# Asking for two spectrum buffers earlier: every buffer of the split weights moves by 2,112 bytes

## The chip, the cores and the metric

The kernel runs on one core of a Trainium2 chip. The metric is the device time of one launch in microseconds (us), as the median of several runs. Time within a run comes from one profiled execution, whose records give each instruction's engine, start and length. The engines are PE (TensorE: matmuls, with PEld its weight loads), DVE (VectorE), ACT (ScalarE), POOL (GpSimd) and SP (SyncE, which issues most of the DMAs). The on-chip memory SBUF has 128 partitions, and an address below is a byte offset within each partition.

## What is computed

The reference, cut to what matters (8 batches, 8 heads, 576 tokens, 64 values a head, 32 packed queries, model width 512):

```python
def sm_attn(qq, kk, vv):
    s = scale * qq @ kk.T;  a = exp(s - max(s));  return (a / (sum(a) + 1e-9)) @ vv

p_packed = sm_attn(p, k, v)                 # 32 packed rows per head
x = sm_attn(q, p_packed, p_packed)          # heads joined: [8, 576, 512]
u = x + real(fft(fft(x, axis=tokens), axis=width))
un = (u - mean(u)) / sqrt(var(u) + 1e-6)
out = u + relu(un @ w_ch1) @ w_ch2          # 512 -> 2048 -> 512
```

## The kernel before

**Two parts.** `front(b)` does attention, the two Fourier transforms (as matmuls with tables of waves) and the residual for batch b. `ffn` does the feed-forward part for a tile of 512 tokens. There are 8 batches and 9 tiles of tokens. `front(0)` runs ahead; from then on the front of the next batch is cut into steps (`yield`) that `step` puts between the halves of the current tile's feed-forward.

**The feed-forward part.** A tile has 16 steps over the hidden width, j = 0 to 15, and each has two halves, which this text calls up and down:

- `up(j)`, matmul line 804: 128 hidden rows for 512 tokens. PE loads a 128x128 piece of the weights (`wr_h` or `wr_l`) and streams 512 columns of the tokens past it (`uh` or `ul`): 4 pieces of the width times 3 products, 12 matmuls into one bank of PSUM (`ph`).
- `down(j - 1)`, matmul line 822: PE loads a 128x128 piece of the hidden rows (`hh` or `hl`) and streams 512 columns of weights past it (`wr_h` or `wr_l`): 4 groups of tokens times 3 products, 12 matmuls, each three of them into one of the four banks `acc0` to `acc3`.

Every number is kept as a sum of two parts of type fp32r, a high and a low one, so each product is made of three matmuls (high by high, high by low, low by high). Of the two operands of a matmul this text calls the one that is loaded the *loaded* operand, and the one that streams past it the *streamed* one. The split weights are the streamed operand of a down matmul and the loaded operand of an up matmul. In numbers, 9 tiles x 16 steps x 24 matmuls are 3,456 matmuls with 512 columns (the first `up` of the first tile is cut into two halves of 256 columns), 1,728 on each line.

**What feeds it.** `wsplits` splits the weights anew for every tile: ACT casts 128x512 of them to `wr_h` (line 99), POOL subtracts to get `wr_l` (line 100). Six buffers with the tag `wr` take turns. After an `up`, ACT writes `hh` (line 811) and DVE `hl` (line 812), two buffers each. `uh` and `ul` are one buffer each per tile of tokens, with 2,048 bytes for each of the four pieces.

**Where a buffer lies.** The pool `work` gives each tag its place in SBUF in the order in which tags are first asked for, one behind the other, each rounded up to 32 bytes. All of it happens while the program is written; nothing is placed while it runs. The order of the first requests around the change is: `xh`, `oh`, `fh`, `fl`, `xl`, `ol` (batch 0's folded attention weights), `yr0` and `yr1` in `wave_split` (line 565), `wr` in `wsplits` (line 776; the first request comes from `waves_of`, line 579), `spec0` and `spec1` in `spectrum` (line 591), then `ln` (`un`), `ul`, `hh`, `hl`. The tag `uh` comes much earlier, because `folded` (line 471) uses it for batch 0 under the name `f`. A `spec` buffer takes 1,032 bytes (258 columns), rounded up to 1,056; all buffers of the feed-forward part take multiples of 2,048.

`first_values` (line 603) is the step "X" of batch 0's order of work. It stands before the step "P1", in which `waves_of` runs `wave_split`, and so before the first requests for `yr0` and `wr`.

Of the kernel before, what the change touches and what calls it, by code (L numbers as in the profile page):

```python
# [9 lines left out]
F32 = mybir.dt.float32  # L10
# [7 lines left out]
P = 128  # L18
# [33 lines left out]
N2 = 258  # L52
# [25 lines left out]
def tile_kernel(ctx, tc, kpT, qT, v, w1, w2, tabs, tabR, tabB, tabT, sel, ident_d, out):  # L78
# [5 lines left out]
    work = ctx.enter_context(tc.tile_pool(name="work", bufs=2))  # L84
# [7 lines left out]
    def bank(name):  # L92
        nbank[0] += 1
        if nbank[0] % 7 < 4 and spare:
            return psf.tile([P, 512], F32, tag=spare[nbank[0] % 7], name=name)
        return ps.tile([P, 512], F32, tag="ps", name=name)
# [136 lines left out]
    def three(o, lh, ll, rh, rl, first, last):  # L233
        nc.tensor.matmul(o, lh, rh, start=first, stop=False)  # L234
        nc.tensor.matmul(o, lh, rl, start=False, stop=False)  # L235
        nc.tensor.matmul(o, ll, rh, start=False, stop=last)  # L236

    def front(b):
# [342 lines left out]
        def spectrum(t, par):  # L581

            pz = bank("pz")
            k0, off = (0, 0) if par is not None else (P, rows.start)
            pars = (0, 1) if par is None else (par,)
            for i, q in enumerate(pars):
                w = slice(KW * q + k0 - off, KW * q + k0 - off + P)
                three(pz[:, :N2], tbh[t][:, w], tbl[t][:, w], yh[t][:, q, :], yl[t][:, q, :], i == 0, False)
            k0 = KW * par if par is not None else k0
            nc.tensor.matmul(pz[:, :N2], tbr[t][:NRC[t], k0 - off:k0 - off + P], yr[t][:NRC[t]], start=False, stop=True)  # L590
            sb = work.tile([P, N2], F32, tag=f"spec{t}", name=f"spec{t}", bufs=1)
            nc.scalar.copy(sb, pz[:, :N2])
            return sb

        def value(ah, al, w):
            px = bank("px")
            for g in range(2):
                three(px[:, g * 256:(g + 1) * 256], ah[g][:, w], al[g][:, w], bdh[g], bdl[g], True, True)
            return px

        early = []

        def first_values():
            early.extend(value(h, l, slice(1, 256, 2)) for h, l in ((xh, xl), (oh, ol)))

        parts = {"S": lambda _: scores(0, 1), "s": scores, "q": queries, "U": lambda _: queries(0, 1), 
                 "t": turned_scores, "p": packed, "c": on_diagonal, "d": packed_parts, "l": packed_split,
                 "v": turned_queries, "X": lambda g: first_values() if b == 0 else turned_scores(0, 1), "e": less_one, "m": less_mean, "g": values_spectrum,
                 "G": values_products, "T": values_turned, "z": values_split, "a": weights, "w": scaled, "b": upright,
                 "f": folded, "r": folded_rest, "h": folded_parts, "x": values_rest, "P": waves_of,  # L610
# [46 lines left out]
        if b == 0:  # L657

            pq = None
            for c in range(2):  # L660
                px = early if c == 0 else [side_value(n, c) for n in range(2)]
                AB = spectrum(0, c), spectrum(1, c)
                if c == 1:
                    yield
                    for key in ((b, "E", 0), (b, "O", 0)):
                        rows_of(key, *pq)
                        statistics(key)
                        yield
                else:
                    yield  # L670
                pq = sums(c, lambda n: px[n], *AB)
# [6 lines left out]
        else:  # L678
            for c in range(2):
                A, Bs = spectrum(0, c), spectrum(1, c)  # L680
                yield
                pe, qe = sums(c, lambda n: side_value(n, c), A, Bs)
                for key in ((b, "E", c), (b, "O", c)):
                    rows_of(key, pe, qe)
                for key in ((b, "E", c), (b, "O", c)):
                    statistics(key)
                yield (None, "rest")[c]

        kr = (b // 2, "R")
        if b % 2 == 0:  # L690
            new_u(kr)
        rows = slice(0, D) if b % 2 == 0 else slice(D, P)
        A, Bs = spectrum(0, None), spectrum(1, None)
        yield
        px = value(fh, fl, slice(FA - rows.start, FA - rows.start + P))
# [180 lines left out]
    tiles = [(i, keys[i:i + 4]) for i in range(0, len(keys), 4)]  # L876

    gen0 = front(0)
    cur = Turned(tiles[0][1])
    ready, splits = [], wsplits()  # L880
# [38 lines left out]
    for t, (first, tk) in enumerate(tiles):  # L919

        gen = front(t + 1) if t + 1 < B else iter(())
        ended = []

        def step(i):

            next_step()

            k = i + 2 * LEAD
            if i in (0, 2):
                next(rest, None)  # L930
            elif not ended and next(gen, None) == "rest":
                ended.append(gen)
            if t == 0 and i > 0 and k <= 2 * NJ:
                joined((k - 1) // 2, (k - 1) % 2)
                if 8 < k + 2 < 2 * NJ:
                    fetch((k + 2) // 2, (k + 2) % 2)
            if t == 0 and k < 2 * NJ:
                halves_of(k // 2, k % 2)
            assert i < 2 * NJ - 1 or t + 1 >= B or ended

        nxt = Turned(tiles[t + 1][1]) if t + 1 < len(tiles) else None

        with tc.manual_schedule(engines=MANUAL):
            ffn(first, cur, step, nxt, t + 1 >= B, t + 1)
        cur, rest = nxt, gen
# [112 lines left out]
```

## Time and profile before

| | us |
|---|---|
| median of 3 runs | 998.75 (997.57 to 1001.8) |
| the profiled execution, whole | 999.18 |
| its span, first to last instruction | 997.4 |
| PE busy | 963.9 (97%) |
| weight loads (PEld) | 781.5 (78%) |
| DVE, ACT, POOL busy | 552.7, 473.9, 462.9 |

Matmuls are pipelined: a record of 390 to 400 ns runs from a matmul's start until its last result, while the next one starts some 230 ns after it. What a matmul costs in a row of matmuls is read from the distance between starts, and not from its mean length. In the chain of waits, a piece like "PE acc L822 x24" is a row of 24 matmuls, and its length divided by 24 is that distance.

### The profile page before, as it was taken

Reading aid. Unit: us, or ns where it says so; the run is one execution under the profiler, and the core shown is the slowest. Engines: PE = TensorE matmul, PEld = TensorE weight load, DVE = VectorE, ACT = ScalarE, POOL = GpSimd, SP = SyncE. Lnnn points to the kernel's source line nnn. Section 1 sums busy time; section 2 is a strip of 40 time slices with the busy share of each in tenths; the row PEclk is TensorE's granted clock in tenths of the full one; section 3 lists DMA queues with packets and bytes.
Section 4 is the critical chain, followed back from the end, with each engine's and each line's share of the span. In section 5 each row is a group of like instructions: output and inputs, shape, how many; then the busy total and the mean of one; then the engine's idle time right before and its main releaser. Section 6 shows DMA issues by size and latency. Waiting matters only on the chain.

```text
span 997.4 us, 14993 instructions
## 1 busy us (share of the span) xinstructions
PE 963.9 (97%) x5588; PEld 781.5 (78%) x5588; DVE 552.7 (55%) x1153; ACT 473.9 (48%) x957; POOL 462.9 (46%) x405
## 2 busy tenths in 40 slices
PE   4589999999999999999999999999999999999998
PEld 2567788788877887788878887788778888888886
DVE  5877865576546845585547654684549551123111
ACT  4687775444544445444534454444543443344331
POOL 2456544554445433643455444543455354444442
PEclk9799999999999999999999999999999999999999
DMA  9336543300140003101320024002310010011001
GB/s 367 105 131 193 156 134 103 112 1 1 47 143 26 1 14 128 49 1 47 104 86 1 16 77 143 1 2 60 129 48 1 22 65 1 1 35 50 1 1 43
DMA packets 28169, 65.93 MB, mean 66 GB/s; under 512 B 5494, under 2 KB 12992, under 8 KB 28096
## 3 DMA queue, kind: packets, MB, share of 16 engines
q1 hardware_dynamic: 27264, 63.79, 19.4%
q0 software_dynamic: 832, 1.18, 0.5%
q8 instruction: 44, 0.72, 0.3%
q14 instruction: 29, 0.24, 0.1%
HBM read 48.70 MB, written 9.44 MB: 58 GB/s over the span
## 4 chain that ended last, share of the span: by engine, by line
PE 90%; DVE 4%; ACT 3%; DMA 1%; issue 1%; POOL 1%; DVEq 0%; ACTq 0%; POOLq 0%
PE acc L822 38%; PE ph L804 38%; PE po L323 1%; PE py L236 1%; PE py L234 1%; PE py L235 1%; PE s L266 1%; PE px L236 1%; PE px L234 1%; PE px L235 1%; PE e1tp L300 1%; PE pz L234 1%; PE pz L236 1%; PE pz L235 1%; PE s2T L266 1%
## 5 line engine op out<-in xcount | busy, mean ns | idle before, releaser
L100 POOL TENSOR_TENSOR wr_l<-w1f,wr_h 128x512 fp32r<-128x512 f32 x144 | 192.6, 1337 | 294.2 <-ACT wr_h L99 254.8
L812 DVE SCALAR_TENSOR_TENSOR hl<-ph,hh 128x512 fp32r<-128x512 f32 (+1 forms) x145 | 99.6, 687 | 346.0 <-ACT hh L811 345.8
L100 POOL TENSOR_TENSOR wr_l<-w2f,wr_h 128x512 fp32r<-128x512 f32 x144 | 188.6, 1309 | 172.8 <-ACT wr_h L99 172.2
L804 PE MATMUL ph<-uh,wr_h 128*128 128x512 f32 (+1 forms) x580 | 230.3, 398 | 4.0 <-DVE hl L812 2.6
L822 PE MATMUL acc<-wr_h,hh 128*128 128x512 f32 x576 | 228.7, 397 | 0.0
L822 PE MATMUL acc<-wr_l,hh 128*128 128x512 f32 x576 | 228.2, 396 | 0.0
L822 PE MATMUL acc<-wr_h,hl 128*128 128x512 f32 x576 | 228.0, 396 | 0.0
L804 PE MATMUL ph<-uh,wr_l 128*128 128x512 f32 (+1 forms) x580 | 227.3, 392 | 0.0
L804 PE MATMUL ph<-ul,wr_h 128*128 128x512 f32 (+1 forms) x580 | 221.8, 391 | 0.0
L811 ACT ACTIVATE hh<-ph 128x512 fp32r<-128x512 f32 (+1 forms) x145 | 86.4, 596 | 215.7 <-PE ph L804 214.9
L804 PEld LDWEIGHTS ph<-uh,wr_h 128*128 128x128 f32 x580 | 109.1, 188 | 40.2 <-ACT gh L99 6.0
L822 PEld LDWEIGHTS acc<-wr_h,hl 128*128 128x128 f32 x576 | 108.1, 188 | 26.1
L804 PEld LDWEIGHTS ph<-uh,wr_l 128*128 128x128 f32 x580 | 108.9, 188 | 24.7
L822 PEld LDWEIGHTS acc<-wr_h,hh 128*128 128x128 f32 x576 | 108.1, 188 | 24.7
L822 PEld LDWEIGHTS acc<-wr_l,hh 128*128 128x128 f32 x576 | 108.1, 188 | 23.9
L804 PEld LDWEIGHTS ph<-ul,wr_h 128*128 128x128 f32 x580 | 108.7, 188 | 22.5
L99 ACT CAST wr_h<-w1f 128x512 fp32r<-128x512 f32 x144 | 89.1, 618 | 60.8 <-PE acc L822 53.9
L99 ACT CAST wr_h<-w2f 128x512 fp32r<-128x512 f32 x144 | 88.3, 613 | 13.4 <-PE acc L822 7.6
L234 PE MATMUL py<-gh,fh 128*128 128x258 f32 (+2 forms) x96 | 28.2, 294 | 13.6 <-ACT fh L99 13.6
L213 ACT ACTIVATE junk<-ubuf,stat 128x512 f32<-128x512 f32 x36 | 25.6, 714 | 24.9 <-DVE stat L209 24.9
L100 POOL TENSOR_TENSOR gl<-turned,gh 128x516 fp32r<-128x516 f32 x16 | 24.6, 1537 | 26.9 <-ACT gh L99 26.9
L217 POOL TENSOR_TENSOR stat<-stat,mhalf 128x1 f32<-128x1 f32 x36 | 24.3, 690 | 11.5 <-DVE stat L216 11.5
(186 smaller groups left out, 1229.5 us busy)
## 6 DMA issues: line engine op xcount, KB each, us to landing
kp<-kpT SPq DMA_DIRECT2D x16, 608.0 KB, 3.9
out<-ubuf SPq DMA_DIRECT2D x36, 256.0 KB, 2.1
vt<-v SPq DMA_DIRECT2D x14, 640.0 KB, 4.8
wst<-w SPq DMA_DIRECT2D x17, 512.0 KB, 3.9
qt<-qT SPq DMA_DIRECT2D x14, 576.0 KB, 5.1
raw<-flip SPq DMA_DIRECT2D x208, 32.0 KB, 1.8
ubuf<-w SPq DMA_DIRECT2D x9, 512.0 KB, 3.8
w1f<-w SPq DMA_DIRECT2D x3, 512.0 KB, 11.3
```

Source lines behind the costliest of these rows:

```text
L99: nc.scalar.copy(hi, src)
L100: (lo_eng or nc.vector).tensor_tensor(lo, src, hi.bitcast(F32), ALU.subtract)
L213: nc.scalar.activation(junk, u, AF.Square, bias=st[:, 1:2], scale=1.0, accum_out=st[:, 2:3])
L217: nc.gpsimd.tensor_tensor(st[:, 2:3], st[:, 2:3], mhalf, ALU.pow)
L234: nc.tensor.matmul(o, lh, rh, start=first, stop=False)
L235: nc.tensor.matmul(o, lh, rl, start=False, stop=False)
L236: nc.tensor.matmul(o, ll, rh, start=False, stop=last)
L266: nc.tensor.matmul(res[g][c][at, :w.stop - w.start], lhs(g, h), rhs(g, h, w), start=True, stop=True, tile_position=(r, h * NPK))
L804: nc.tensor.matmul(o[:, t], l[:, c * P:(c + 1) * P], r[:, c, t], start=(n == 0), stop=(n == 11))
L811: nc.scalar.activation(hh[:, t], o[:, t], AF.Relu)
L812: nc.vector.scalar_tensor_tensor(hl[:, t], o[:, t], 0.0, hh[:, t].bitcast(F32), ALU.max, ALU.subtract)
L822: nc.tensor.matmul(acc[i], l[:, w], r, start=(j == 0 and k == 0), stop=(j == NJ - 1 and k == 2))
```

## The change

`first_values` now asks for the two `spec` buffers, before `yr` and `wr` have been asked for, and keeps them in a dictionary; `spectrum` takes the buffer from there at its first use for each of the two, and asks the pool itself from then on, as before.

```diff
-            sb = work.tile([P, N2], F32, tag=f"spec{t}", name=f"spec{t}", bufs=1)
+            sb = specs.pop(t, None) or work.tile([P, N2], F32, tag=f"spec{t}", name=f"spec{t}", bufs=1)
             nc.scalar.copy(sb, pz[:, :N2])
             return sb
...
-        early = []
+        early, specs = [], {}
 
         def first_values():
+
+            specs.update((t, work.tile([P, N2], F32, tag=f"spec{t}", name=f"spec{t}", bufs=1)) for t in range(2))
             early.extend(value(h, l, slice(1, 256, 2)) for h, l in ((xh, xl), (oh, ol)))
```

No engine has an instruction more or less, and none stands in another place or waits for something else; only addresses differ. As the two programs are built, these are the addresses (bytes in a partition) and what is left of them after division by 2,048 and by 128:

| buffer | before | mod 2,048 | mod 128 | after | mod 2,048 | mod 128 |
|---|---|---|---|---|---|---|
| `uh` (4 x 2,048) | 161408 | 1664 | 0 | 161408 | 1664 | 0 |
| `spec0`, `spec1` | 204608, 205664 | 1856, 864 | 64, 96 | 190208, 191264 | 1792, 800 | 0, 32 |
| `yr0`, `yr1` | 190208, 191264 | 1792, 800 | 0, 32 | 192320, 193376 | 1856, 864 | 64, 96 |
| `wr` (6 x 2,048) | 192320 | 1856 | 64 | 194432 | 1920 | 0 |
| `un`, `ul`, `hh`, `hl` | 206720 and on | 1920 | 0 | 206720 and on | 1920 | 0 |

So of the feed-forward operands only the six `wr` buffers move. They then lie a multiple of 2,048 bytes from `ul`, `hh` and `hl`; `uh` lies 256 bytes off that grid before and after.

## Prediction

> **What bounds the kernel now.** I read the page first, then the chain of waits, then PE's waits, and last single starts of matmuls on the timeline. From the page, the span and the engines:
>
> ```profile
> span 997.4 us, 14993 instructions
> PE 963.9 (97%) x5588; PEld 781.5 (78%) x5588; DVE 552.7 (55%) x1153; ACT 473.9 (48%) x957; POOL 462.9 (46%) x405
> PE 90%; DVE 4%; ACT 3%; DMA 1%; issue 1%; POOL 1%; DVEq 0%; ACTq 0%; POOLq 0%
> PE acc L822 38%; PE ph L804 38%; PE po L323 1%; PE py L236 1%; PE py L234 1%; PE py L235 1%; PE s L266 1%; PE px L236 1%; PE px L234 1%; PE px L235 1%; PE e1tp L300 1%; PE pz L234 1%; PE pz L236 1%; PE pz L235 1%; PE s2T L266 1%
> ```
>
> The third and fourth lines are the chain that ended last, by engine and by line: 90% of it is PE, and the two feed-forward lines hold 38% each, some 760 of the 997.4 us. Next, who keeps PE waiting, and how busy the engines are in the middle (busy us of PE, PEld, DVE, ACT and POOL with their instructions, then the granted clock):
>
> ```profile
> PE py L234 <- ACT fh L99: 13.6, 1, 13.6
> PE s1t L266 <- DMA kp<-kpT: 4.7, 1, 4.7
> PE ph L804 <- DVE hl L812: 2.6, 3, 1.4
> ...
> 500.00:600.00 100.00, 100.00 (x578) 81.81 (x577) 63.45 (x132) 45.21 (x90) 50.21 (x42) 1.00 0.14 42
> ```
>
> The longest wait, 13.6 us, happens once, the next, 4.7 us, once as well, and no feed-forward line waits more than 2.6 us in all. In the middle PE has no idle time, at the full clock, while DVE, the busiest of those that feed it, is idle for a third of it. So the time of this kernel is the number of matmuls times the distance between their starts, and only what changes that distance can show. How many they are:
>
> ```profile
> L804 PE MATMUL ph<-uh,wr_h 128*128 128x512 f32 (+1 forms) x580 | 230.3, 398 | 4.0 <-DVE hl L812 2.6
> L822 PE MATMUL acc<-wr_h,hh 128*128 128x512 f32 x576 | 228.7, 397 | 0.0
> L822 PE MATMUL acc<-wr_l,hh 128*128 128x512 f32 x576 | 228.2, 396 | 0.0
> L822 PE MATMUL acc<-wr_h,hl 128*128 128x512 f32 x576 | 228.0, 396 | 0.0
> ```
>
> The down line has 3 x 576 = 1,728 matmuls, the up line the same number to within a dozen. Their mean length, 396 to 398 ns, says nothing about the distance. That stands in the longest pieces of the chain:
>
> ```profile
> 898.59 5.60 PE acc L822 x24
> 904.19 5.51 PE ph L804 x24
> ```
>
> 24 down matmuls take 5.60 us, 233.3 ns each; 24 up matmuls take 5.51 us, 229.6 ns each. That is the row on which the prediction rests: two kinds of matmul with the same columns, the same types, the same engine, without waits, and 3.7 ns between them. Inside one step (an up and the down behind it, starts in the first column; the rows left out are the matmuls between):
>
> ```profile
> 940.13 0.39 PE L804 MATMUL ph<-uh,wr_h 128*128 128x512 f32 x1
> ...
> 941.29 0.39 PE L804 MATMUL ph<-uh,wr_l 128*128 128x512 f32 x1
> ...
> 942.66 0.39 PE L804 MATMUL ph<-uh,wr_l 128*128 128x512 f32 x1
> 942.89 0.39 PE L822 MATMUL acc<-wr_h,hh 128*128 128x512 f32 x1
> 943.12 0.40 PE L822 MATMUL acc<-wr_l,hh 128*128 128x512 f32 x1
> 943.36 0.39 PE L822 MATMUL acc<-wr_h,hl 128*128 128x512 f32 x1
> 943.59 0.40 PE L822 MATMUL acc<-wr_h,hh 128*128 128x512 f32 x1
> 943.83 0.39 PE L822 MATMUL acc<-wr_l,hh 128*128 128x512 f32 x1
> ...
> 945.69 0.39 PE L804 MATMUL ph<-uh,wr_h 128*128 128x512 f32 x1
> ```
>
> From 940.13 to 942.89 are 12 up intervals, 230.0 ns each; the last six before 942.66, from 941.29 on, are 228.3 ns each, so an up starts slower and settles. From 942.89 to 945.69 are 12 down intervals, 233.3 ns. Not every up is that quick. In the middle of the run there is this one:
>
> ```profile
> 535.54 0.40 PE L804 MATMUL ph<-uh,wr_h 128*128 128x512 f32 x1
> ...
> 538.11 0.39 PE L804 MATMUL ph<-uh,wr_l 128*128 128x512 f32 x1
> ```
>
> Its 11 intervals are 233.6 ns each, the down's rate. So there are two rates, about 229 and about 233.4 ns; the down shows only the slow one, the up both.
>
> **The change, part by part.** No instruction is added, taken away or moved, so there is no cost of that kind. What can change is what an instruction costs at its new addresses.
>
> *The down matmuls.* They stream `wr`, which lies 64 bytes past a multiple of 128 now, and load `hh` or `hl`, which lie on one. The quick up matmuls stream `uh` and `ul`, which lie on a multiple of 128. What else tells the two apart is that a down changes its bank of PSUM every three matmuls, but its rows show no step there: from the third matmul at 943.36 to the fourth, in the next bank, it is 0.23 us, as it is from the first to the second. So I take the place of the streamed operand as the likeliest reason, and after the change it is on a multiple of 128 everywhere. Then the down runs at the rate of the piece with 24 up matmuls: 1,728 / 24 = 72 pieces, each 5.60 - 5.51 = 0.09 us shorter, 6.5 us. All of it is on the path, since PE is what everything waits for. Upper bound: all matmuls at the settled 228.3 ns, which is (233.3 - 228.3) x 1,728 = 8.6 us in the down and (229.6 - 228.3) x 1,728 = 2.2 us in the up, together 10.9 us. Lower bound under this reason: only half of the downs get there, as an up also runs slow at times: 3.2 us. I take 6.5, the value that a row of 24 shows.
>
> *The up matmuls.* They load `wr` and stream what hasn't moved. If it is the loaded operand's place that counts, they lose what they have: 72 pieces at 5.60 in place of 5.51, 6.5 us more at most, and less by those ups that are slow already. Under the reason above it is nothing.
>
> *The other readers and writers.* ACT and POOL write `wr`, at new addresses:
>
> ```profile
> L99 ACT CAST wr_h<-w2f 128x512 fp32r<-128x512 f32 x144 | 88.3, 613 | 13.4 <-PE acc L822 7.6
> L100 POOL TENSOR_TENSOR wr_l<-w2f,wr_h 128x512 fp32r<-128x512 f32 x144 | 188.6, 1309 | 172.8 <-ACT wr_h L99 172.2
> ```
>
> A step of 5.56 us (940.13 to 945.69) needs two of each, 2 x 0.61 us of ACT and 2 x 1.31 us of POOL, so both could get slower by half and would still hide behind PE. `yr` is the streamed operand of one line:
>
> ```profile
> L590 PE MATMUL pz<-yr,tbr x48: 280/284/288, 42.5 to 817.0; 101*128 101x258 f32 x24, 99*128 99x258 f32 x24
> ```
>
> 48 matmuls by a difference of the size seen above, 3.7 ns, are 0.2 us either way. `spec` is read by DVE, a third of whose time is free. Together I set these at nothing, with 0.2 us to either side.
>
> *A rule that speaks against the change.* The Trainium skill, page "SBUF — State Buffer", section "Who interferes with whom", says that PE has two independent read ports, one for the streamed operand and one for the weight load, and that PE never waits on anyone; it names no price for where an operand starts. By that rule the sum would be zero. The trace agrees in that PE has no idle time in the 100 us above, with DVE, ACT and POOL at work for 63, 45 and 50 us of them; whether it also holds for an operand's place no row of one program can show.
>
> *The sum.* The profiled execution took 999.18 us, its span 997.4 and 1.8 around it. 997.4 - 6.5 + 1.8 = 992.7. The median of the three runs is 0.43 below that execution, so the forecast is 992.3, rounded to 992.
>
> **The rivals.** A difference of about 0.5%, 5 us, is what a measurement of this kernel can tell from none.
>
> *The place is not the reason.* The two rates could be two ways in which the same loop of load and stream falls into step, as the slow up at 535.54 suggests: its addresses are those of any other up, but for which of the six `wr` buffers it loads. Then the down would be slow for another reason (three products in a bank and not twelve, or what it waits for at its first matmul), the rates stay, and the time is 998.75, between 997 and 1001. This is also the rule of the page above. For it speaks the slow up; against it that no down in the rows above is quick.
>
> *The change doesn't do what it says.* `uh` stays 256 bytes off the grid, and two of three up matmuls stream it. If all operands had to be on one grid, only the down and the `ul` matmuls would change. It gives a part of the first sum, 3 us or so, and I count it with no change.
>
> *Slower: what counts is how near the loaded operand lies to the streamed one.* In a down the two lie 64 bytes apart modulo 512, in an up 192 bytes (`wr` behind `uh`) or 64 bytes short of a whole 512 (`wr` behind `ul`); the down is the slow one. Afterwards a down and the `ul` matmuls have them at the same place modulo 512. If near is slow, the down gains nothing, and the up falls to the down's rate: +6.5 us at most, 1005, and some 1003 with the slow ups left out. If "the same place" costs one step more than 64 bytes, the downs add 72 x 0.09, another 6.5 us, 1012. It decides from the point where the weight load, 188 ns of each interval, is held up by the stream beside it:
>
> ```profile
> L822 PEld LDWEIGHTS acc<-wr_h,hl 128*128 128x128 f32 x576 | 108.1, 188 | 26.1
> ```
>
> For it speaks the order of the two rates; against it that the load, at 188 ns, has some 40 ns to spare in 230.
>
> *Much faster: what an interval has beyond its columns goes.* Four matmuls with 258 columns give the price of a column:
>
> ```profile
> 77.77 0.28 PE L418 MATMUL pg<-basis,pph 128*128 128x258 f32 x1
> ...
> 78.25 0.39 PE L822 MATMUL acc<-wr_h,hh 128*128 128x512 f32 x1
> ```
>
> They are 0.48 / 4 = 120 ns apart; from 258 to 512 columns it is 110 ns more, 0.43 ns a column, which leaves 8 ns of an interval that no column explains. If all of it went, 3,456 x 8 ns = 28 us, 971. The Trainium skill, page "TensorE: Matmul & The Clock Gate", section "Back-to-back issue gap", gives 512 columns as 512 / 2.4 + 2.5 = 215.7 ns; by that the intervals of 231.5 ns on average would have 54 us to lose, 944. No interval of the rows above is near it.
>
> **How the numbers follow.** The streamed operand's place: 0.45, faster except for its end below 5 us, which I set at 0.03 of the 0.45. Much faster: 0.03. No effect, or only a part of one: 0.30. Slower: 0.22, of which 0.05 stays below 5 us. So faster is 0.45 - 0.03 + 0.03 = 0.45, same 0.30 + 0.03 + 0.05 = 0.38, slower 0.17. The range goes from 986 (the sum with 10.9 us, 987.9, and the 2 us by which runs differ) to 1004, in which the slower rival's first price lies to half. Outside are the much faster case, the price of 1012 and the upper half of the first one, together under 0.2. The likeliest case alone holds 987 to 996.
>
> **What would show it.** Right: a piece of 24 down matmuls in the chain takes 5.50 to 5.52 us, and 24 up matmuls no more than 5.51. The step that took 5.56 us takes 5.50. PE's waits on the feed-forward lines stay below 5 us. Wrong: down pieces still at 5.60 (the place of the streamed operand doesn't matter); up pieces at 5.60 (the loaded operand's place, or nearness, does); both near 5.5 or 5.6 with another time than the sum, which would put the difference outside of these matmuls, above all into a longer start-up or waits for POOL.

## The result, and the profile after

The changed kernel takes 985.01 us (median of 4 runs, 984.27 to 989.62), the kernel before 998.42 us beside it. The ratio is 0.9869, with a 95% interval from 0.9831 to 0.9907. The direction is the one forecast; the gain, 13.4 us, is twice the 6.5 us of the sum, and the time lies 1 us below the low end of the range.

The span and the engines of the profiled execution (984.27 us), from the page of the changed kernel:

```profile
span 982.5 us, 14993 instructions
PE 949.3 (97%) x5588; PEld 780.8 (79%) x5588; DVE 551.1 (56%) x1153; ACT 473.8 (48%) x957; POOL 466.0 (47%) x405
```

The span fell by 14.9 us (997.4 - 982.5) and PE's busy time by 14.6 (963.9 - 949.3), with the same 5,588 matmuls. Hardly anything else gave or took time: the other engines are busy as long as before within 3.1 us, and PE's longest waits are the same within 0.5 us. Who kept PE waiting, from the changed kernel's waits (us in all, times, longest):

```profile
PE py L234 <- ACT fh L99: 13.6, 1, 13.6
PE s1t L266 <- DMA kp<-kpT: 4.6, 1, 4.6
...
PE ph L806 <- DVE hl L814: 2.1, 3, 1.0
```

So the matmuls stand closer together. The chain of waits of the changed kernel, the same two pieces as before (start, length; the up line is 806 now, the down line 824):

```profile
885.71 5.44 PE acc L824 x24
891.15 5.45 PE ph L806 x24
```

The down went from 5.60 to 5.44, the up from 5.51 to 5.45. By these pieces that is 72 x 0.16 = 11.5 us and 72 x 0.06 = 4.3 us, 15.8 in all, of which the span shows 14.9. A piece is one undisturbed row, though, in which no other matmuls stand between. PE's busy time by line over the whole run says how the gain is divided (the third number; the down before and after, then the up before and after):

```profile
0.00:998.00 998.00, 428.14 (x1728) 320.41 (x1728) 0.99 0.20 66
0.00:998.00 998.00, 418.74 (x1728) 320.53 (x1728) 0.99 0.20 66
0.00:998.00 998.00, 425.58 (x1740) 321.57 (x1740) 0.99 0.20 66
0.00:998.00 998.00, 420.54 (x1740) 321.03 (x1740) 0.99 0.20 66
```

The down gained 9.4 us and the up 5.0, together 14.4 of the 14.9. The up gained more than its piece says; before, some ups were slower than 5.51 us for 24, as the one at 535.54 was. Why the down gained less is below. One step on the timeline of the changed kernel, an up and the down behind it:

```profile
931.80 0.39 PE L806 MATMUL ph<-uh,wr_h 128*128 128x512 f32 x1
...
934.52 0.39 PE L824 MATMUL acc<-wr_h,hh 128*128 128x512 f32 x1
...
937.24 0.39 PE L806 MATMUL ph<-uh,wr_h 128*128 128x512 f32 x1
```

Both halves take 2.72 us, 226.7 ns a matmul; before, they took 2.76 and 2.80. In such rows there are no two rates any more, and the common one is below both. Where work of the next batch stands between two halves, the matmuls behind it are slower, and the gain is smaller. A down of the changed kernel behind 80 small matmuls (the rows left out are matmuls of the same down):

```profile
499.90 1.73 PE L323 MATMUL po<-vt,e1T 128*32 128x64 f32 x80
...
501.90 0.40 PE L824 MATMUL acc<-wr_l,hh 128*128 128x512 f32 x1
...
504.21 0.39 PE L824 MATMUL acc<-wr_h,hl 128*128 128x512 f32 x1
```

Its ten intervals from 501.90 to 504.21 are 231.0 ns each, not 226.7. Before, the same down (508.20 to 510.53) had 233.0: it gained 2 ns an interval, a down in an undisturbed row 6.6. Others settle on the way, as this down behind small matmuls of line 236:

```profile
473.10 0.39 PE L824 MATMUL acc<-wr_h,hh 128*128 128x512 f32 x1
...
474.49 0.39 PE L824 MATMUL acc<-wr_h,hh 128*128 128x512 f32 x1
...
475.85 0.39 PE L806 MATMUL ph<-uh,wr_h 128*128 128x512 f32 x1
```

Its first six intervals are 231.7 ns each, its last six 226.7.

### The profile page after: what moved, and what is told of

The parts are those of the page before. It is cut to its first block, busy times and chain, and to the rows that moved or that the text cites. A ratio compares the mean times of both kernels' runs of the same rounds, so it can differ in the third digit from the quotient of the medians.

```text
span 982.5 us, 14993 instructions
## 1 busy us (share of the span) xinstructions
PE 949.3 (97%) x5588; PEld 780.8 (79%) x5588; DVE 551.1 (56%) x1153; ACT 473.8 (48%) x957; POOL 466.0 (47%) x405
## 4 chain that ended last, share of the span: by engine, by line
PE 90%; DVE 5%; ACT 2%; issue 1%; DMA 1%; POOL 1%; DVEq 0%; POOLq 0%; ACTq 0%
PE ph L806 39%; PE acc L824 38%; PE po L323 1%; PE py L236 1%; PE py L234 1%; PE py L235 1%; PE s L266 1%; PE px L236 1%; PE px L234 1%; PE px L235 1%; PE e1tp L300 1%; PE pz L234 1%; PE pz L236 1%; PE pz L235 1%; PE s2T L266 1%
## 5 line engine op out<-in xcount | busy, mean ns | idle before, releaser
L100 POOL TENSOR_TENSOR wr_l<-w2f,wr_h 128x512 fp32r<-128x512 f32 x144 | 191.1, 1327 | 164.9 <-ACT wr_h L99 158.1
L824 PE MATMUL acc<-wr_h,hh 128*128 128x512 f32 x576 | 226.2, 393 | 0.0
L824 PE MATMUL acc<-wr_l,hh 128*128 128x512 f32 x576 | 225.2, 391 | 0.0
L824 PE MATMUL acc<-wr_h,hl 128*128 128x512 f32 x576 | 225.2, 391 | 0.0
```

The costliest lines, as they stand in the source:

```text
L100: (lo_eng or nc.vector).tensor_tensor(lo, src, hi.bitcast(F32), ALU.subtract)
L824: nc.tensor.matmul(acc[i], l[:, w], r, start=(j == 0 and k == 0), stop=(j == NJ - 1 and k == 2))
```

## The experiments

The theory after the result: what counts is the distance between the operand that is loaded and the one that streams, and it costs nothing if it is a multiple of some number of bytes. The first rival is the forecast's reason, the place of the streamed operand itself (or of both) on a multiple of 128. The second is that `spec` and `yr`, which moved too, have to do with it. All kernels but `pads_only` and `uh_grid` are the changed kernel with one unused buffer in the pool, which pushes what is asked for later; all have the instructions of the changed kernel, at other addresses. The table gives, modulo 256, how far the loaded operand lies behind the streamed one in each.

| kernel | down: `hh` / `hl` behind `wr` | up: `wr` behind `uh` / `ul` | us | ratio to before, 95% |
|---|---|---|---|---|
| before | 64 | 192 / 192 | 998.4 to 999.1 | 1 |
| changed | 0 | 0 / 0 | 985.01 | 0.9869 [0.9831, 0.9907] |
| `all_64` | 0 | 0 / 0 | 985.95 | 0.9865 [0.985, 0.988] |
| `tail_256` | 0 | 0 / 0 | 985.31 | 0.9867 [0.9836, 0.9897] |
| `uh_grid` | 0 | 0 / 0 | 984.26 | 0.9852 [0.9832, 0.9871] |
| `pads_only` | 0 | 0 / 0 | 985.69 | 0.9871 [0.9849, 0.9892] |
| `hl_64` | 0 / 64 | 0 / 0 | 991.82 | 0.9929 [0.9904, 0.9955] |
| `tail_192` | 192 | 0 / 64 | 993.29 | 0.9944 [0.9927, 0.9961] |
| `hh_64` | 64 | 0 / 0 | 996.31 | 0.9976 [0.9967, 0.9986] |
| `tail_128` | 128 | 0 / 128 | 997.64 | 0.9987 [0.9976, 0.9997] |
| `tail_64` | 64 | 0 / 192 | 999.69 | 1.0 [0.9987, 1.0013] |
| `tail_32` | 32 | 0 / 224 | 1000.19 | 1.002 [1.0006, 1.0034] |

**The place of an operand or the distance: `all_64`.** 64 bytes ahead of `uh` move all five operands together.

```diff
                 if g == 0:
+                    work.tile([P, 16], F32, tag="pad0", name="pad0", bufs=1)
                     fs[None] = work.tile([P, 4, 512], F32, tag="uh", name="f", bufs=1)...
```

> All five feed-forward operands moved on by 64 bytes together: the distances between them are those of the changed kernel, but each now lies 64 bytes past a multiple of 128. If the streamed operand's own place counts (a multiple of 128, the forecast's reason), or that of both operands, every matmul loses its quick rate: pieces of 24 at 5.51 to 5.60 us, 992 to 998 us. If only the distance between the loaded and the streamed operand counts, nothing changes: 5.44 us for 24 of either kind, 985 us.

The last two long pieces of its chain (the down line is 825 here, the up line 807):

```profile
887.76 5.44 PE acc L825 x24
893.20 5.44 PE ph L807 x24
```

Every operand lies 64 bytes past a multiple of 128, and both kinds run as quickly as in the changed kernel. That an operand lies on a multiple of 128 isn't what counts; the forecast's reason falls.

**The distance alone: `tail_64`.** `wr` and `uh` stay; `un`, `ul`, `hh`, `hl` move on by 64.

```diff
                 hi = work.tile([P, DM], F32R, tag="wr", name="wr_h", bufs=6)
+                if not ready and (n, j) == (0, 0):
+                    work.tile([P, 16], F32, tag="pad2", name="pad2", bufs=1)
```

> Only ul, hh and hl (and un) move on by 64 bytes; uh and wr stay on multiples of 128. If the streamed operand's place counts, the down matmuls (they stream wr) stay at 5.44 us for 24, and of the up matmuls the third that streams ul gets slower: about 987 us. If the distance counts, the down is 64 bytes apart as it was before, 5.60 us for 24, and the up matmuls with uh stay quick while those with ul don't: 992 to 996 us.

```profile
899.57 5.60 PE acc L826 x24
905.17 5.54 PE ph L808 x24
```

The whole gain is gone: 5.60 for the down, though it still streams `wr` from a multiple of 128, and 5.54 for the up, though only one of its three products is off. The time was expected at 996 us at most and came to 999.69; what was expected of the up, that only the matmuls with `ul` lose, is 5.49 at most (a third of 0.16 more), and 5.54 was measured. All three products at 192, as before the change, took 5.51: one of three off costs the up no less than all three.

**Which distances: `tail_128`, `tail_32`, `tail_256`, `tail_192`.** The same buffer with 128, 32, 256 and 192 bytes (`[P, 32]`, `[P, 8]`, `[P, 64]`, `[P, 48]`).

> ul, hh and hl move on by 128 bytes: all operands lie on multiples of 128, but the two operands of a down lie 128 bytes apart modulo 256, 512 and 2,048. If a multiple of 128 is what counts, for one operand or for the distance: 5.44 us for 24 of either kind, 985 us. If the distance must be a multiple of 256 or more: the down at 5.5 to 5.6 us, 990 to 996 us.

> ul, hh and hl move on by 32 bytes. If the streamed operand's place counts, the down stays at 5.44 us for 24. If the distance counts, a down 32 bytes apart leaves 5.44: at 5.60 us if any distance but a multiple of 128 is slow, between the two if 32 bytes cost less than 64.

> ul, hh and hl move on by 256 bytes, so the two operands of a down lie 256 bytes apart modulo 512 and 2,048, and wr and ul too. If a distance of a multiple of 256 is enough: 5.44 us for 24 of either kind, 985 us. If it must be a multiple of 512 or of 2,048: the down near 5.6 us, 994 us or more.

> ul, hh and hl move on by 192 bytes, the last step of 64 below 256. If only multiples of 256 are quick: 5.55 to 5.60 us for 24, 994 to 1000 us. If the cost falls off again towards 256: between 5.44 and 5.55.

The pieces with 128, 32, 256 and 192 bytes, in this order:

```profile
895.80 5.59 PE acc L826 x24
901.40 5.55 PE ph L808 x24
```

```profile
897.83 5.59 PE acc L826 x24
903.42 5.55 PE ph L808 x24
```

```profile
888.40 5.44 PE acc L826 x24
893.84 5.44 PE ph L808 x24
```

```profile
893.58 5.50 PE acc L826 x24
899.09 5.52 PE ph L808 x24
```

A multiple of 128 is not enough, a multiple of 256 is. In `tail_128` all operands lie on multiples of 128 and both kinds are slow, which speaks against the forecast's reason a second time. In between, 32, 64 and 128 bytes cost the same within 0.02 us for 24, and 192 bytes, at 5.50, less than half of it. The last value agrees with the row of before on which the prediction rests: there an up had its loaded operand 192 bytes behind the streamed one modulo 256 (5.51), and a down 64 bytes (5.60).

**Does `uh` have to lie on the grid of 2,048 bytes: `uh_grid`.** `fh`, `fl`, `spec` and `yr` are asked for ahead of `uh`, 16,640 bytes in all, which moves it to 178048, 1920 modulo 2,048.

```diff
                 if g == 0:
+                    sooner["fh"] = [work.tile([P, FW], F32R, tag="fh", name="fh") for _ in range(2)]
+                    sooner["fl"] = [work.tile([P, FW], F32R, tag="fl", name="fl") for _ in range(2)]
+                    sooner["spec"] = [work.tile([P, N2], F32, tag=f"spec{t}", name=f"spec{t}", bufs=1) for t in range(2)]
+                    sooner["yr"] = [work.tile([P, N2], F32R, tag=f"yr{t}", name="yr", bufs=1) for t in range(2)]
                     fs[None] = work.tile([P, 4, 512], F32, tag="uh", name="f", bufs=1)...
```

> uh moves onto the grid of the others, 2,048 bytes or multiples of it from them; nothing else of the feed-forward part moves. If 256 bytes is the period: no change from the changed kernel, 985 us and 5.44 us for 24. If 2,048 is: the up gets quicker by what uh still costs, below 5.44 us for 24 up matmuls.

```profile
887.31 5.44 PE acc L829 x24
892.75 5.44 PE ph L811 x24
```

No gain that can be told: 984.26 beside 985.01 us, with overlapping intervals. So 256 bytes is enough, and 2,048 is a multiple that happens to be the buffers' size. That 256 bytes is the period is taken from the distances tried; in a whole row of matmuls, 96, 160 and 224 were not.

**One half alone: `hh_64`.** 64 bytes ahead of `hh` leave the up as it is.

```diff
+            if first == 0 and j == 0:
+                work.tile([P, 16], F32, tag="pad3", name="pad3", bufs=1)
             hh = work.tile([P, 512], F32R, tag="hh", name="hh")
```

> Only hh and hl move on by 64 bytes; uh, ul and wr keep their distances. If what counts is the distance of the two operands of one matmul: the up stays at 5.44 us for 24 or near it, the down goes to 5.60 as before, 72 x 0.16 = 11.5 us at most, 994 to 997 us. If one operand off the grid disturbs all matmuls: the up gets slow too, 999 us, as with ul, hh and hl moved.

```profile
895.97 5.60 PE acc L826 x24
901.56 5.47 PE ph L806 x24
```

In these pieces the down pays all of it, the up nearly nothing. In a down the streamed operands are `wr` buffers alone, on one grid, and the loaded ones `hh` and `hl`, on one grid too; only the distance of the one kind to the other is new. 72 x (5.60 - 5.44) = 11.5 us on top of 985.0 is 996.5; 996.31 were measured. That this fits so well is partly luck: by PE's busy time over the whole run the down loses 9.5 us (428.27 against 418.74) and the up 2.6 (423.11 against 420.54). An up whose own operands are at distance 0 starts slowly behind a down that runs slowly (rows left out are of the same up):

```profile
909.67 0.39 PE L806 MATMUL ph<-uh,wr_h 128*128 128x512 f32 x1
...
910.83 0.39 PE L806 MATMUL ph<-uh,wr_l 128*128 128x512 f32 x1
...
912.42 0.40 PE L826 MATMUL acc<-wr_h,hh 128*128 128x512 f32 x1
```

Its first five intervals are 232 ns each, its last seven 227.

**One load of three: `hl_64`.** The same buffer ahead of `hl` instead (`pad4`).

> Only hl moves on by 64 bytes: one load of three in a down is off, and none in an up. If each matmul with an operand off pays for itself, a third of the down's loss: 24 down matmuls at 5.44 + 0.16 / 3 = 5.49 us, some 988 to 989 us. If one load off spoils the whole down, 5.60 us and some 995 us, as with hh and hl both moved.

```profile
893.42 5.54 PE acc L826 x24
898.96 5.45 PE ph L806 x24
```

5.54 is neither of the two: 0.10 of the 0.16 us for one load in three. So an operand off the grid costs about twice its share. One down of this run shows which interval pays:

```profile
904.25 0.39 PE L826 MATMUL acc<-wr_h,hh 128*128 128x512 f32 x1
904.48 0.39 PE L826 MATMUL acc<-wr_l,hh 128*128 128x512 f32 x1
904.49 0.19 PEld L826 LDWEIGHTS acc<-wr_h,hl 128*128 128x128 f32 x1
904.71 0.40 PE L826 MATMUL acc<-wr_h,hl 128*128 128x512 f32 x1
904.94 0.39 PE L826 MATMUL acc<-wr_h,hh 128*128 128x512 f32 x1
...
905.40 0.40 PE L826 MATMUL acc<-wr_h,hl 128*128 128x512 f32 x1
905.64 0.39 PE L826 MATMUL acc<-wr_h,hh 128*128 128x512 f32 x1
...
906.09 0.40 PE L826 MATMUL acc<-wr_h,hl 128*128 128x512 f32 x1
906.33 0.39 PE L826 MATMUL acc<-wr_h,hh 128*128 128x512 f32 x1
...
906.79 0.40 PE L826 MATMUL acc<-wr_h,hl 128*128 128x512 f32 x1
907.02 0.39 PE L806 MATMUL ph<-uh,wr_h 128*128 128x512 f32 x1
```

The four intervals that start with an `hl` matmul are 235 ns each, the other eight 229. This bears on a rival that all other kernels leave open: that what counts is the distance between the stream and the load that runs beside it, which is the load of the *next* matmul (`hl` is loaded at 904.49, beside the matmul of 904.48). Then the interval before the `hl` matmul would be the slow one, and it isn't. The slow one is that of the matmul whose own two operands are off; in it, too, the loads go back from `hl` to `hh`, so a cost of changing from one offset to another isn't told apart from it. By the sum 72 x 0.10 = 7.2 us, 992.2; 991.82 were measured. The up of `tail_64` (5.54, one of its two streamed operands off) also costs more than its share, and that it costs no less than three at 192 speaks for such a cost of changing; no run separates it.

**The same gain without the change: `pads_only`.** The kernel before, with its order of requests, and two unused buffers.

```diff
+                if not ready and (n, j) == (0, 0):
+                    work.tile([P, 16], F32, tag="pad1", name="pad1", bufs=1)
                 hi = work.tile([P, DM], F32R, tag="wr", name="wr_h", bufs=6)
...
+            if i == 0:
+                work.tile([P, 48], F32, tag="pad2", name="pad2", bufs=1)
             self.un[i] = work.tile([P, DM], F32, tag="ln", name="un")
```

> The kernel before, with its order of requests, and two unused buffers of 64 and 192 bytes, ahead of wr and ahead of un, which bring all feed-forward operands to distances of multiples of 256. If the distance is the cause: 985 us, 5.44 us for 24 of either kind. If it was the place of spec and yr, which stay where they were: 998 to 999 us.

```profile
885.30 5.44 PE acc L826 x24
890.74 5.44 PE ph L808 x24
```

It is the changed kernel's time, 985.69 us, with `yr` at its old address and `spec` behind `wr` as before (64 bytes further on, since the first unused buffer stands ahead of it). The second rival falls: the new order is worth nothing but the distances that it makes.

## Why the prediction was right in direction and wrong in reason and size

*What bounds the kernel.* Right. The time is the number of matmuls times their distance, and the gain came out of almost nothing else: 14.4 us on the two feed-forward lines, of 14.9 us of span.

*The step that failed: "I take the place of the streamed operand as the likeliest reason ... Then the down runs at the rate of the piece with 24 up matmuls".* Both halves of it were wrong. The place is not the reason (`all_64`, `tail_128`), the distance between the loaded and the streamed operand is (`tail_64`, `hh_64`), counted modulo 256 bytes (`tail_128`, `tail_256`). And the up's rate was no floor. I took 5.51 us for 24 as the quick state because it was the quicker of two rows, but both rows of before had their operands off, by 192 and by 64 bytes, and nothing in that profile showed what 0 costs. The term of 6.5 us in the down measured 9.4 over the whole run, and 72 x 0.16 = 11.5 by the pieces from which it was made. That the direction came out is in part luck: the move that puts `wr` on a multiple of 128 also brings its distance to the other operands to a multiple of 256.

*The up: "Under the reason above it is nothing".* It gained 5.0 us over the whole run, 72 x 0.06 = 4.3 by the pieces. Under the right reason the same move of `wr` had to show on both lines, since it is an operand of both. The upper bound of 10.9 us, made with the settled 228.3 ns, failed for the same cause: 226.7 ns is what both came to in undisturbed rows.

*The other readers and writers.* Right. Two rows of the changed kernel's page answer to those shown of before, POOL's subtraction and a weight load of the down:

```profile
L100 POOL TENSOR_TENSOR wr_l<-w2f,wr_h 128x512 fp32r<-128x512 f32 x144 | 191.1, 1327 | 164.9 <-ACT wr_h L99 158.1
...
L824 PEld LDWEIGHTS acc<-wr_h,hl 128*128 128x128 f32 x576 | 108.1, 188 | 23.1
```

POOL takes 1327 ns in place of 1309, hidden behind PE, which has no idle time in the middle. The weight load takes its 188 ns as before.

*The rule that PE never waits on anyone.* The Trainium skill, page "SBUF — State Buffer", section "Who interferes with whom", gives PE two independent read ports, and the page "TensorE: Matmul & The Clock Gate", section "Step-by-step: what each phase is for", says that loading the next weights doesn't take read bandwidth from the running matmul. Here a shift of one operand by 64 bytes makes 24 matmuls take 5.60 in place of 5.44 us (`hh_64`), so for these fp32r matmuls the measurement decides against the two reads being independent. That PE waits for another engine is not shown by this. I had given that rule's result, or only a part of an effect, 0.30.

*The rivals.* "How near the loaded operand lies to the streamed one" named the right quantity with the wrong sign: I took the same place for no better than 64 bytes, and it is the best of those tried. "`uh` stays 256 bytes off the grid" was true of the description and cost nothing (`uh_grid`). That the two rates are only ways of falling into step is half right: behind other work the rate can take several matmuls to settle, as the down at 473.10 shows, and may not get there in twelve, as at 501.90; but what it settles to is set by the distance. "Much faster" looked below both rates, at 8 ns of an interval that no column explains: from 231.5 ns on average to 226.7 some 5 of them went, and I had given it 0.03.

*The range.* It reached to 986 by 10.9 us and the scatter of runs. With two rates in view that could not be explained, the lower end ought to have allowed a third rate below both. An estimate that the rows of before would have allowed: half of those 8 ns is 28 / 2 = 14 us, some 985. It is made after the result, and nothing in that profile said that half would go.

*What stays open.* Why 256 bytes is enough, and what in the path of loads and streams is shared, isn't settled by these runs; that two reads meet in the same part of the memory was only thought of. Why some ups of before, as the one at 535.54, ran at 233.6 ns with the same distances as the quicker ones isn't known either, nor what a change of offset from one matmul to the next costs. Nor is it known whether the other matmuls of the kernel (258 columns, operands at all kinds of offsets) have something to gain; it wasn't tried.

## What to carry to other kernels

When the same kind of matmul shows two distances between starts and no wait explains it, look at the addresses of the two operands as the program was built, before looking for a schedule. In this kernel the operand that is loaded and the one that streams had to lie a multiple of 256 bytes apart, and 256 bytes of unused buffers did that as well as a new order of requests did: 1.3% of the time for nothing else. And a rate that a profile shows is no floor as long as every row of it has the same fault; a range needs room for a better one. Last, a price taken from one undisturbed row, times the number of rows, is an estimate: here it put the down at 11.5 us, and 9.4 came.

## What the runs showed of the hardware that was not expected

- The time between starts of fp32r matmuls with 512 columns, in undisturbed rows, depends on the two operands' distance modulo 256 bytes: 226.7 ns at 0 (5.44 us for 24), 229 ns at 192 (5.50), 233 ns at 32, 64 and 128 (5.59 to 5.60). Moving all operands by 64 bytes changed nothing (`all_64`).
- One load of three that is off costs about two thirds of what all three cost (`hl_64`, 5.54 us), and the interval of the matmul with that load holds most of it, 235 ns against 229.
- The quick rate isn't always there at once: behind 80 small matmuls ten intervals of a down of the changed kernel are 231.0 ns long, and not 226.7; behind others a down reaches 226.7 after six intervals of 231.7.
- The weight loads' own length, 188 ns in the down before and after, shows nothing of it; only the distance between starts does.
